# Gathers of V that wait for the logits' transposes, and a new set of engine orders

## The chip, the cores and the metric

The kernel runs on one core of one Trainium2 chip. The metric is the device time of one execution in microseconds (us); less is better. Five engines work side by side, each with its own in-order queue of instructions: TensorE (PE), ScalarE (ACT), VectorE (DVE), GpSimd (POOL) and SyncE (SP), which here only issues DMAs. They wait for one another, and for transfers, through semaphores.

## The reference, cut to what matters

```
xn = layernorm(x)                                   # x: 2048 rows of 512
# A: attention over 8 positions, each 2 rows apart, 32 heads of 16
q, k, v = split(xn @ wqkv)
logits[s,h,w] = 16**-0.5 * q[s,h] . k[s - 2*w, h]    # masked where s - 2*w < 0
A = (sum_w softmax_w(logits)[s,h,w] * v[s - 2*w, h]) @ wo
# B: a gated MLP with a product over the sequence
z = gelu(xn @ w_in);  z1 = z[:, :896];  z2 = layernorm(z[:, 896:])
g = w_sp @ z2 + b_sp                                 # w_sp: 2048 x 2048
B = (z1 * g) @ w_out
out = x + A + B                                      # bf16
```

## The kernel before, in words

All work is cut into some 800 named tasks. `build_kernel` declares them with what each reads and writes; from this come the dependencies. The order in which each engine runs its tasks is a written-out list, `ORDERS`, one for each of the five queues. An engine takes its tasks strictly in this order and, before each, waits for the tasks of other engines and the transfers that it depends on. A task that waits therefore holds up everything behind it on its engine.

The sequence has 16 blocks of 128 rows, in four groups `j` of four blocks. The stages, as PE sees them:

- **Front.** Per block: layer norm on DVE and POOL (`bnst`, `bnag`, `rstd`, `norm`), its transpose (`xTr` on PE, or `xTd`, a DMA transpose), then the products `z2_b_h` (the second half of `w_in`, halves h of 448 columns), `Qj_c`, `Kj_c` and `Vb`. ACT takes them out of PSUM: `z2g` (gelu), `z2s` (squares for the second layer norm), `QKe` and `halo` (Q and K), `Ve`. The V blocks go to a scratch tensor in DRAM, `vscr` (`Vw`, issued by SP).
- **Logits.** For each group, DVE multiplies Q with eight shifted copies of K (`prod`, `padd`), PE sums over the head (`lgj_0`, L707), and ACT copies the result to `stage` (`lgej`, L745). When all four groups are there, SP issues four DMA transposes `lgT0` to `lgT3` (L756) from `stage` to `attn`. `stage` lies on slots 15 to 22 of the buffer `Ve`.
- **z1.** Meanwhile PE makes the 32 half products `z1_b_h` (L807), through three pairs of PSUM banks, each freed by an ACT gelu `z1g` (L818). The z2 blocks are normalised in place, most on DVE (`zn`, L855), the last four on ACT (`zn12` to `zn15`, L851).
- **Softmax.** DVE and ACT compute it in two halves (even and odd blocks): `sm1` to `sm3` (maximum, L768 to L774), `ssub` (L780), `sexp` (L783, ACT), `sz1` to `sz3` (sum), `sln` and `srec` (ACT), `sattn` (L794). `sm1_0` is the first reader of `attn`.
- **Gate.** `w_sp @ z2` is done for eight pairs `i` of blocks with seven products instead of eight (Strassen's way): `P1_i` to `P7_i` (L930), each 8 matmuls of 128 x 448. They need sums of the z2 blocks made on DVE (`T1` L874, `T3` L877, `T2` L879, `T4` L881) and, for each pair, sums of the transposed `w_sp` blocks (`S13_i` L902, `S2_i` L905, `S4_i` L908); the blocks come by DMA transposes `wTi_h` (L892, SP). ACT copies the partial sums (`fk`, `S5`, `S2e`, `Sc`, `S3e`, `g11` to `g22`; L936, L958), and DVE multiplies with z1 (`u`).
- **V.** DVE multiplies the attention weights with the V rows (`pvb`, L1000) and adds up (`pva`, `pvc`). The V rows come back from `vscr` by nine gathers, `ldVp_k` (parity p, first slot k; L983), issued on ACT's queue. `ldV0_0` brings nine slots (1152 KB), `ldV1_7` eight (1024 KB), the others one or two.
- **Output.** DMA transposes `OTd` and `uT`, then `out_b` on PE (4 matmuls L1037 and 7 matmuls L1041), with x added through PSUM (`ldxr`, `os`), then `fin` and `st`.

PSUM ties the stages together: `P1_0` writes a bank that `z1g3` must have emptied, `P5_0` one of `z1g1`, `z1_5` one of `z1g11`.

Of the kernel before, what the change touches and what calls it, by code (L numbers as in the profile page):

```python
# [207 lines left out]
warm xTr0 fill0 z2_0_0 xTr1 z2_0_1 z2_1_0 xTr2 z2_1_1 xTr3 z2_2_0 z2_2_1 z2_3_0 Q0_0 K0_0 z2_3_1 K0_1 Q0_1 Q0_3
K0_2 Q0_2 K0_3 V0 V3 V1 V2 V4 V7 Q1_0 K1_0 V6 V5 K1_2 Q1_2 K1_1 Q1_1 Q1_3 z2_5_1 K1_3 z2_4_1 z2_4_0 z2_5_0
z2_6_1 z2_6_0 lg0_0 V9 V8 z2_7_1 z2_7_0 Q2_1 V11 K2_1 V10 Q2_0 K2_0 Q2_2 K2_2 z2_8_1 z2_8_0 K2_3 Q2_3 z2_11_0  # L210
z2_9_0 z2_9_1 z2_11_1 z2_10_1 z2_10_0 Q3_0 K3_0 V12 lg1_0 V15 K3_3 Q3_3 Q3_1 V13 K3_2 V14 K3_1 z2_14_1 z2_14_0
Q3_2 z2_12_1 z2_12_0 z2_13_0 z2_13_1 lg2_0 z2_15_0 z1_2_1 z2_15_1 z1_2_0 z1_0_0 z1_4_1 z1_4_0 z1_0_1 z1_8_1
# [8 lines left out]
actprime ldw_in2a_1 ldw_in2b_1 ldx3 xTe0 xTe1 z2g0 xTe2 xTe3 z2g1 z2g2 QKe0_0 halo0_0 z2g3 halo0_1 z2s0 QKe0_1
halo0_2 z2s1 QKe0_2 QKe0_3 z2s2 Ve3 halo0_3 Ve0 Ve1 Ve2 Ve7 Ve4 Ve6 Ve5 zm0 QKe1_0 QKe1_2 halo1_1 halo1_0
halo1_2 QKe1_1 z2s3 halo1_3 QKe1_3 z2g4 z2g5 z2s4 Ve9 Ve8 z2g6 lge0 z2g7 halo2_1 Ve11 QKe2_1 Ve10 z2s5 QKe2_0
z2s6 zm1 halo2_0 halo2_2 z2g8 halo2_3 QKe2_2 z2s7 QKe2_3 z2g11 z2g9 z2g10 QKe3_0 Ve12 Ve15 lge1 z2s8 z2s9 Ve13
# [5 lines left out]
S2e_4 srec1 fin0_0 os4_0 S3e_4 S5_4 g22_3 st0_0 Sc_4 g22_4 ldV1_6 ldxr10 g11_4 fin4_0 ldV1_2 g21_4 g11_5 S5_5  # L230
ldV1_4 os8_0 S2e_5 fin6_0 os10_0 S3e_5 st6_0 Sc_5 g12_4 fk_6 ldV1_0 S5_6 ldxr14 fin8_0 g12_5 st4_0 os12_0 g21_5
fin10_0 S2e_6 st10_0 os14_0 g22_5 ldxr15 S3e_6 st8_0 fin12_0 fk_7 os15_0 ldxr9 fin14_0 ldxr13 os13_0 st12_0 Sc_6
g21_6 ldxr11 g11_6 fin15_0 st14_0 S2e_7 g11_7 g22_6 ldxr7 g12_6 fin13_0 S5_7 S3e_7 os11_0 st15_0 st13_0 Sc_7
os9_0 ldxr5 ldxr3 g12_7 fin11_0 os7_0 fin9_0 os5_0 g21_7 g22_7 st11_0 fin7_0 ldxr1 os3_0 st7_0 st9_0 fin5_0
# [28 lines left out]

# [15 lines left out]
def build_kernel(nc, A_x, A_wqkv, A_wo, B_x, B_w_in, B_w_sp, B_b_sp, B_w_out, out,   # L279
# [82 lines left out]
    with ExitStack() as es:  # L362
# [391 lines left out]
        def lg_transposes():  # L754
            for n in range(4):
                dma("sp", (lambda n: lambda e: e.dma_start_transpose(  # L756
                    AC(off["attn"] + 1024 * n, [[128, 8], [1, 128]]), A("stage", 1024, 1024 * n)))(n),
                    128 * 1024 * 2, ("lgT", n), reads=["stage"] + [("lgs", j) for j in range(NJ)],
                    writes=[("attn", b) for b in range(4 * n, 4 * n + 4)], name="lgT%d" % n, xbar=True)
# [219 lines left out]
        def ld_v(par, k0, n):  # L979
            s0 = k0 + 8 * par  # L980
            src = bass.AP(tensor=vscr.tensor, offset=vscr.offset + (par + 2 * k0 + 2) * 512,
                          ap=[[16 * 512, 128], [1024, n], [1, 512]])
            dma("act", lambda e: e.dma_start(AC(off["Ve"] + 512 * s0, [[512, n], [1, 512]]), src), 128 * 512 * 2 * n,  # L983
                ("Ve", s0), reads=[("vscr", i) for i in range(-1, NB)], writes=[("Ve", s0 + i) for i in range(n)],
                name="ldV%d_%d" % (par, k0), prio=LOW)
# [201 lines left out]
```

## Time and profile before

| what | value |
|---|---|
| time, median of 3 runs | 232.52 us (231.87 to 236.08) |
| time of the profiled execution | 232.16 us |
| span of its profile | 230.4 us |
| PE busy | 221.3 us, 96% |
| DVE busy | 204.2 us, 89% |
| ACT busy | 147.6 us, 64% |
| POOL busy | 35.2 us, 15% |
| granted TensorE clock | full in every slice |
| DMA | 34.18 MB, mean 148 GB/s |

The span is from the first to the last instruction of the profile; the time has 1.8 us more around it. Times in the rows below are microseconds from the start of the span. A row of the order of time gives start, duration, engine, line and operation; a count such as x64 says that so many instructions in a row are merged. "SPq" and "ACTq" are the queues that issue DMAs. In brackets stands the idle time of the engine before the row and what ended it. Matmuls are pipelined: the end of one overlaps the start of the next.

### The profile page before, as it was taken

The page shows a single profiled execution, that of the slowest core. Times are in us where ns is not written, and L with a number is a line of the kernel's source. Part 1 is how long each engine was busy: PE and PEld are TensorE (multiplying, and loading weights), DVE is VectorE, ACT ScalarE, POOL GpSimd, SP SyncE. Part 2 cuts the span into 40 slices and gives each one's busy share as a digit, 9 for nine tenths or more (in the row PEclk, how much of TensorE's full clock was granted, in tenths as well). Part 3 has the DMA queues.
Part 4 walks back from the last instruction along what each step waited for, and adds up shares of the span by engine and source line. Part 5 has one row for each costly group of instructions (what it writes and reads, how often), then busy time and mean ns, then how long its engine had stood idle before and what let it go on. Part 6 is the DMA issues. An engine that isn't in the chain of part 4 may idle for free.

```text
span 230.4 us, 3073 instructions
## 1 busy us (share of the span) xinstructions
PE 221.3 (96%) x1128; PEld 115.6 (50%) x1142; DVE 204.2 (89%) x208; ACT 147.6 (64%) x258; POOL 35.2 (15%) x40
## 2 busy tenths in 40 slices
PE   7999999999999999949999899999999999999995
PEld 3454454455444776724455455454545444545443
DVE  4889999999999999639999999699999999999710
ACT  2579587788799796877993266349155525347562
POOL 2437304720370502011120000000000000000000
PEclk9999999999999999999999999999999999999999
DMA  6974631664309702970769952999999667827782
GB/s 190 318 243 48 182 90 49 177 145 87 84 20 163 176 1 48 170 216 24 182 190 170 254 137 55 167 216 232 211 227 193 169 120 175 154 68 171 165 180 68
DMA packets 84767, 34.18 MB, mean 148 GB/s; under 512 B 69280, under 2 KB 84400, under 8 KB 84752
## 3 DMA queue, kind: packets, MB, share of 16 engines
q1 hardware_dynamic: 74464, 23.78, 50.8%
q10 hardware_dynamic: 9408, 8.74, 13.2%
q0 software_dynamic: 880, 1.47, 2.2%
q8 instruction: 9, 0.15, 0.3%
q14 instruction: 6, 0.05, 0.1%
HBM read 12.98 MB, written 4.21 MB: 75 GB/s over the span
## 4 chain that ended last, share of the span: by engine, by line
PE 84%; DMA 8%; SPq 2%; DVE 2%; ACT 2%; issue 1%; DVEq 0%
PE ps L930 30%; PE ps L807 16%; PE ps L669 12%; PE ps L1041 10%; PE ps L646 6%; PE ps L1037 6%; DMA arena<-arena 5%; DMA arena<-in_B_w_sp_dram 3%; PE ps L567 2%; SPq L756 2%; ACT arena L818 1%; PE ps L707 1%; PE ps L619 1%; DVE arena L902 1%; DVE arena L879 0%
## 5 line engine op out<-in xcount | busy, mean ns | idle before, releaser
L930 PE MATMUL ps<-arena 128*128 128x448 bf16 x448 | 87.1, 352 | 4.0 <-DVE arena L855 3.2
L930 PEld LDWEIGHTS ps<-arena 128*128 128x128 bf16 x448 | 43.6, 98 | 46.2 <-issue 3.6
L807 PE MATMUL ps<-arena 128*128 128x448 bf16 x256 | 50.9, 353 | 0.1
L807 PEld LDWEIGHTS ps<-arena 128*128 128x128 bf16 x256 | 30.5, 121 | 18.6 <-issue 0.8
L694 DVE TENSOR_TENSOR arena<-arena 128x4096 bf16<-128x4096 bf16 x16 | 36.3, 2280 | 0.8 <-ACT arena L677 0.7
L1000 DVE TENSOR_TENSOR arena<-arena 128x4096 bf16<-128x4096 bf16 x16 | 36.2, 2286 | 0.2
L936 ACT ACTIVATE arena<-ps 128x448 bf16<-128x448 f32 x32 | 16.9, 539 | 28.7 <-PE ps L930 24.0
L818 ACT ACTIVATE arena<-ps 128x896 bf16<-128x896 f32 x32 | 28.7, 915 | 6.9 <-PE ps L807 6.8
L669 PE MATMUL ps<-arena 128*128 128x512 bf16 x123 | 29.2, 379 | 0.3
L1004 DVE TENSOR_TENSOR arena<-arena 128x4096 bf16<-128x4096 bf16 (+1 forms) x16 | 28.1, 1754 | 0.2
L698 DVE TENSOR_TENSOR arena<-arena 128x4096 bf16<-128x4096 bf16 x12 | 27.4, 2287 | 0.1
L1041 PE MATMUL ps<-arena 128*128 128x512 bf16 (+2 forms) x117 | 26.7, 366 | 0.1
L600 POOL TENSOR_TENSOR fpool<-fpool 128x1 f32<-128x1 f32 x16 | 18.9, 1189 | 26.0 <-DVE fpool L598 26.0
L669 PEld LDWEIGHTS ps<-arena 128*128 128x128 bf16 x128 | 14.5, 113 | 13.0 <-issue 0.2
L677 ACT ACTIVATE arena<-ps 128x1024 bf16<-128x1024 f32 x16 | 16.3, 1025 | 2.4 <-PE ps L669 2.4
L1041 PEld LDWEIGHTS ps<-arena 128*128 128x128 bf16 x119 | 11.4, 98 | 12.8
L958 ACT ACTIVATE arena<-arena,fpool 128x448 bf16<-128x448 bf16 x16 | 10.5, 664 | 9.5 <-DVE arena L953 9.5
L1037 PE MATMUL ps<-arena 128*128 128x512 bf16 (+2 forms) x62 | 15.3, 365 | 0.7 <-DMA arena<-arena 0.4
L826 ACT ACTIVATE arena<-arena 128x896 bf16<-128x896 bf16 x16 | 15.3, 955 | 0.1
L646 PE MATMUL ps<-arena 128*128 128x512 bf16 x63 | 15.3, 379 | 0.1
L1050 ACT ACTIVATE arena<-ps 128x512 bf16<-128x512 f32 (+1 forms) x16 | 9.4, 585 | 8.9 <-PE ps L1041 8.9
L843 POOL TENSOR_TENSOR fpool<-fpool 128x4 f32<-128x4 f32 x4 | 9.5, 2384 | 29.5 <-DVE fpool L840 29.5
(76 smaller groups left out, 186.7 us busy)
## 6 DMA issues: line engine op xcount, KB each, us to landing
arena<-in_A_x_dram ACTq DMA_DIRECT2D x17, 128.0 KB, 3.0
vscr<-arena SPq DMA_DIRECT2D x16, 128.0 KB, 1.9
arena<-in_A_x_dram SPq DMA_DIRECT2D x15, 128.0 KB, 2.7
out_dram<-arena ACTq DMA_DIRECT2D x15, 128.0 KB, 2.2
arena<-in_A_wqkv_dram SPq DMA_DIRECT2D x3, 512.0 KB, 4.6
arena<-vscr ACTq DMA_DIRECT2D x6, 256.0 KB, 3.7
arena<-vscr ACTq DMA_DIRECT2D x1, 1152.0 KB, 7.9
arena<-vscr ACTq DMA_DIRECT2D x1, 1024.0 KB, 7.0
```

Of the source, the lines that this page charges most:

```text
L600: T("pool", lambda g: g.tensor_tensor(Fv("rstd", 1, b), Fv("mv", 1, 2 * b + 1), Fv("mhalf", 1), ALU.pow), reads=[("mv", b), "mhalf"], writ ...
L646: last = t.matmul(bank(k + i), AC(off["xnT"] + dc * S + 128 * (b + i), [[1, 128]]), AC(off["wv_raw"] + 512 * dc, [[1, 512]]), start=(dc == ...
L669: last = t.matmul(bank(k + which), AC(off["wqk"] + 1024 * dc + col0, [[4, 128]]), AC(off["xnT"] + dc * S + 512 * j, [[1, 512]]), start=(dc ...
L694: T("dve", lambda v: v.tensor_tensor(pbv, qb, kb, ALU.mult), reads=[("QT", c, j), ("KT", c, j), ("KTpad", c, j)], writes=[("pb", s_)], est ...
L698: T("dve", lambda v: v.tensor_tensor(A("pb", 4096, 4096 * a), A("pb", 4096, 4096 * a), A("pb", 4096, 4096 * b), ALU.add), reads=[("pb", b) ...
L807: last = t.matmul(bank(k + hf, HF), AC(off["xnT"] + dc * S + t0, [[ts, 128]]), AC(off["w_in"] + 1792 * dc + c0, [[1, HF]]), start=(dc == 0 ...
L818: T("act", lambda a: a.activation(A(nm, FH, FH * b).rearrange("p (t n) -> p t n", t=2), PC(512 * k, [[512, 2], [1, HF]]), ACTF.Gelu_apprx_ ...
L930: last = t.matmul(bank(k, HF), AC(lo + 128 * s, [[1, 128]]), mov(s), start=(first and s == 0), stop=(s == 7), skip_group_check=True)
L1000: T("dve", (lambda iv, tv, av: lambda v: v.tensor_tensor(tv, iv, av, ALU.mult))(iv, tv, av), reads=[("attn", pairs[i][b]) for b in blks] + ...
L1004: T("dve", (lambda n: lambda v: v.tensor_tensor(AC(off["Vs"], [[4096, 2], [1, n]]), AC(off["Vs"], [[4096, 2], [1, n]]), AC(off["Vs"] + n, ...
L1037: t.matmul(po, AC(off["OT"] + 512 * os_ + 128 * cc, [[1, 128]]), AC(off["wo"] + 512 * cc + c0, [[1, n]]), start=False, stop=False, skip_gr ...
L1041: last = t.matmul(po, AC(off["uT"] + FH * us + 128 * fc, [[1, 128]]), AC(off["w_out"] + 512 * fc + c0, [[1, n]]), start=False, stop=(fc == ...
```

## The change

Two things change, and no computation is added or removed.

First, every gather `ldV` now also depends on all four transposes `lgT`: each transpose marks a key `lgTd`, which the gathers read. Among the gathers, `ldV1_7` had this dependency already, since its slots are those of `stage`.

Second, all five lists of `ORDERS` are replaced. The lines that bear on the stretch between the last logits and the first gate products are shown; the front and the second half are permuted in the same manner (for example, `out0_0` comes earlier among the products, `P5_2` and `P6_2` stand ahead of `P1_3`, and `ldw_in1` is issued later).

```diff
     pe="""
...
-z1_10_0 z1_6_1 z1_6_0 z1_8_0 z1_10_1 z1_12_1 z1_14_0 z1_14_1 z1_12_0 lg3_0 z1_15_0 z1_13_1 z1_11_1 z1_15_1
-z1_11_0 z1_13_0 z1_9_1 z1_9_0 z1_7_0 z1_7_1 z1_5_1 z1_3_1 z1_3_0 z1_1_1 z1_1_0 z1_5_0 P1_0 P1_1 P2_0 P5_0 P6_0
-P3_0 P6_1 P7_0 P2_1 P4_0 P1_2 P7_1 P5_1 P4_1 P2_2 P3_1 P1_3 P5_2 P6_2 P3_2 P5_3 P7_2 P2_3 P4_2 P6_3 P3_3 P7_3
...
+z1_6_1 z1_8_0 z1_8_1 z1_10_1 z1_10_0 z1_12_1 z1_12_0 z1_14_0 z1_14_1 lg3_0 z1_15_1 z1_15_0 z1_13_1 z1_13_0
+z1_9_1 z1_9_0 z1_7_1 z1_7_0 z1_11_1 z1_11_0 z1_3_1 z1_3_0 z1_1_0 z1_1_1 z1_5_1 P1_0 z1_5_0 P5_0 P2_0 P1_1 P6_0
+P3_0 P7_0 P2_1 P6_1 P5_1 P4_0 P7_1 P3_1 P1_2 P4_1 P2_2 P5_2 P6_2 P1_3 P7_2 P2_3 P4_2 out0_0 P3_2 P6_3 P5_3 P1_4
...
     act="""
...
-z1g10 lge2 z1g14 z1g12 lge3 zm2 z1g15 z1g13 z1g11 bspf z1g9 ldV0_0 z1g7 zn14 zn12 ldxr2 z1g3 zn13 z1g1 zn15 fk_0
-z1g5 sexp0 g11_0 S5_0 fk_1 os2_0 S2e_0 ldV0_11 ldxr8 sln0 srec0 Sc_0 S3e_0 sexp1 g22_0 S2e_1 g21_0 g11_1 fk_2
...
+z1g8 z1g10 z1g12 lge3 z1g14 z1g15 z1g13 zn13 z1g9 zn12 z1g7 ldxr0 z1g11 bspf ldV1_7 z1g3 zn14 zn15 z1g1 fk_0
+ldV0_0 z1g5 sexp0 fk_1 S5_0 S2e_0 sln0 Sc_0 srec0 S3e_0 S2e_1 S5_1 g11_0 g11_1 S3e_1 g12_0 g21_0 fk_2 Sc_1
...
     dve="""
...
-zq3 zv2 padd3_1 prod3_3 padd3_2 padd3_3 zv3 zn0 S13_0 zn2 zn1 smask zn7 zn3 zn11 zn10 S2_0 zn9 T1_0 S4_0 zn6 zn8
-T3_0 zm3 zn4 sm1_0 sm2_0 sm3_0 zn5 ssub0 T2_0 T1_1 T3_1 S13_1 T2_1 S2_1 sz1_0 sz2_0 S4_1 sm1_1 sz3_0 sm2_1 T4_0
-T4_1 sm3_1 ssub1 sattn0 h_0 pv2 pv0 u_0 pva2048_0 S13_2 pva1024_0 pvc0 S2_2 sz1_1 h_1 S4_2 S13_3 S2_3 pv6 sz2_1
...
+padd3_1 zq3 prod3_3 zv3 padd3_2 padd3_3 zn3 zn5 zn0 zn2 S13_1 zn11 zn1 S13_0 zm3 zn6 zn10 zn8 zn9 zn7 T1_0 zn4
+T1_1 sm1_0 T3_0 S2_0 S2_1 sm2_0 sm3_0 T3_1 ssub0 T2_1 S4_0 T2_0 T4_1 sz1_0 sz2_0 sz3_0 sm1_1 T4_0 sm2_1 S4_1
+sm3_1 ssub1 sattn0 h_0 pv0 pv2 pva2048_0 pva1024_0 pvc0 S13_2 S2_2 u_0 S4_2 sz1_1 h_1 pv4 sz2_1 S13_3 pv6 S2_3
...
     sp="""
...
-xTd14 xTd13 wT0_0 Vw8 Vw15 Vw14 wT1_1 wT0_1 Vw13 Vw12 wT1_0 lgT0 lgT3 lgT1 lgT2 wT2_0 wT2_1 wT3_0 wT3_1 uT_2
...
+Vw11 Vw8 wT1_1 ldw_in1 wT0_0 wT0_1 Vw15 Vw12 Vw14 wT1_0 Vw13 lgT0 lgT1 lgT3 lgT2 wT2_0 wT2_1 wT3_0 wT3_1 OTd0
...
@@ lg_transposes
-                    writes=[("attn", b) for b in range(4 * n, 4 * n + 4)], name="lgT%d" % n, xbar=True)
+                    writes=[("attn", b) for b in range(4 * n, 4 * n + 4)] + [("lgTd", n)], name="lgT%d" % n, xbar=True)
@@ ld_v
-                ("Ve", s0), reads=[("vscr", i) for i in range(-1, NB)], writes=[("Ve", s0 + i) for i in range(n)],
+                ("Ve", s0), reads=[("vscr", i) for i in range(-1, NB)] + [("lgTd", i) for i in range(4)], writes=[("Ve", s0 + i) for i in range(n)],
```

In the list of ACT, `ldV1_7` moves from between `fk_5` and `S2e_4` (the middle of the gate stage) to ahead of `z1g3`; `ldV0_0` moves from ahead of `z1g7` to behind `fk_0`.

More of the change, by code (lines that the diff above doesn't have):

```diff
@@ L207 @@
     pe="""
[L208 to L212, printed above, removed]
@@ L218 @@
-out9_0 P4_7 out7_0 out5_0 out3_0 out1_0 out1_1
+warm xTr0 fill0 z2_0_0 xTr1 z2_0_1 z2_1_0 xTr2 z2_1_1 xTr3 z2_2_0 z2_2_1 z2_3_0 z2_3_1 Q0_0 K0_0 Q0_1 Q0_2 K0_2
+K0_1 K0_3 V2 V1 V0 Q0_3 V7 V3 V4 V6 V5 Q1_0 K1_0 K1_1 Q1_2 Q1_1 Q1_3 K1_3 z2_4_1 K1_2 z2_6_1 z2_6_0 z2_4_0
+z2_5_0 z2_5_1 lg0_0 z2_7_1 z2_7_0 V10 V8 V11 V9 K2_0 Q2_0 K2_2 Q2_1 K2_1 Q2_2 K2_3 Q2_3 z2_8_1 z2_8_0 z2_9_0
+z2_9_1 z2_10_1 z2_10_0 z2_11_0 V13 z2_11_1 V14 lg1_0 V12 V15 K3_1 K3_0 Q3_0 K3_2 Q3_1 Q3_3 Q3_2 z2_12_0 z2_12_1
+K3_3 z2_13_1 z2_13_0 z2_14_1 z2_15_1 z2_14_0 lg2_0 z2_15_0 z1_0_0 z1_2_1 z1_0_1 z1_2_0 z1_4_0 z1_6_0 z1_4_1
@@ L219 @@
+P4_7 out9_0 out7_0 out5_0 out3_0 out1_0 out1_1
 """.split(),
     act="""
[L221 to L224, printed above, removed]
@@ L230 @@
[L230 to L234, printed above, removed]
@@ L235 @@
-os1_0 st5_0 fin3_0 st3_0 os1_1 fin1_0 st1_1
+actprime ldw_in2a_1 ldw_in2b_1 ldx3 xTe0 xTe1 z2g0 xTe2 xTe3 z2g1 z2s0 z2g2 z2g3 halo0_0 QKe0_0 QKe0_2 halo0_1
+QKe0_1 Ve2 halo0_2 Ve1 Ve0 QKe0_3 Ve3 halo0_3 Ve5 Ve6 Ve4 QKe1_0 halo1_1 z2s1 halo1_0 QKe1_1 Ve7 QKe1_3 halo1_3
+z2s2 QKe1_2 z2s3 halo1_2 z2g4 z2g6 z2g5 zm0 z2g7 z2s4 Ve8 Ve11 Ve10 Ve9 halo2_0 z2s5 QKe2_0 z2s6 halo2_2 QKe2_1
+lge0 halo2_1 QKe2_2 QKe2_3 halo2_3 z2s7 z2g8 z2g9 z2g10 z2s8 z2g11 Ve14 Ve13 lge1 Ve15 zm1 Ve12 z2s9 QKe3_0
+z2s10 QKe3_1 QKe3_2 z2g12 QKe3_3 z2s11 z2g13 z2s12 z2g14 zm2 z2s13 z2g15 z1g0 z2s14 z1g2 z2s15 z1g4 z1g6 lge2
@@ L236 @@
+g11_4 os10_0 fin8_0 ldV1_2 os12_0 S2e_5 g22_4 S5_5 ldV1_0 ldxr14 S3e_5 g11_5 st6_0 fin10_0 fk_6 ldxr15 g12_4
+fin12_0 st10_0 os14_0 Sc_5 st8_0 ldxr13 ldxr11 g22_5 S5_6 g12_5 g21_5 S2e_6 fin14_0 os15_0 Sc_6 st12_0 S3e_6
+st14_0 ldxr9 g11_6 g22_6 g12_6 os13_0 g21_6 fin15_0 fk_7 ldxr7 S5_7 os11_0 fin13_0 fin11_0 S2e_7 os9_0 st11_0
+ldxr5 ldxr3 S3e_7 st15_0 os7_0 Sc_7 g11_7 st13_0 ldxr1 g12_7 g22_7 g21_7 fin9_0 os5_0 st9_0 fin7_0 st7_0 os1_1
+os3_0 fin5_0 st5_0 os1_0 fin3_0 st3_0 fin1_0 st1_1
 """.split(),
@@ L248 @@
-pva1024_4 pvc4 pv9 pv11 pva2048_5 pva1024_5 S13_7 pvc5 S2_7 pv5 u_11 pv7 pva2048_6 pva1024_6 pvc6 S4_7 h_6 pv1
-pv3 u_7 pva2048_7 pva1024_7 h_7 pvc7 u_3 u_1 fin1_1
+zeros steps0 steps1 bnst0 bnag0 norm0 bnst1 bnag1 xTf0 norm1 bnst2 bnag2 bnst3 bnag3 norm2 bnst5 bnag5 norm3
+bnst7 bnag7 bnst8 bnst6 bnag6 bnst4 bnag8 norm7 bnag4 bnst9 bnst10 norm5 bnst11 norm6 norm4 bnag11 bnag9 bnag10
+prod0_0 prod0_2 prod0_1 norm8 padd0_1 bnst12 bnst13 padd0_2 prod0_3 norm11 bnst15 norm10 bnag15 bnag13 norm9
+bnag12 bnst14 padd0_3 bnag14 prod1_0 prod1_1 zq0 norm13 prod1_2 norm12 zq1 padd1_1 norm14 norm15 padd1_2 prod1_3
@@ new lines @@
+prod2_1 padd1_3 prod2_0 zv0 zv1 padd2_1 prod2_2 prod2_3 padd2_2 zq2 smask padd2_3 prod3_1 prod3_0 zv2 prod3_2
+padd3_1 zq3 prod3_3 zv3 padd3_2 padd3_3 zn3 zn5 zn0 zn2 S13_1 zn11 zn1 S13_0 zm3 zn6 zn10 zn8 zn9 zn7 T1_0 zn4
+T1_1 sm1_0 T3_0 S2_0 S2_1 sm2_0 sm3_0 T3_1 ssub0 T2_1 S4_0 T2_0 T4_1 sz1_0 sz2_0 sz3_0 sm1_1 T4_0 sm2_1 S4_1
+sm3_1 ssub1 sattn0 h_0 pv0 pv2 pva2048_0 pva1024_0 pvc0 S13_2 S2_2 u_0 S4_2 sz1_1 h_1 pv4 sz2_1 S13_3 pv6 S2_3
+pva2048_1 sz3_1 S4_3 u_4 h_2 pva1024_1 pvc1 pv8 pv10 S13_4 pva2048_2 u_8 h_3 pva1024_2 S2_4 pvc2 S4_4 sattn1
@@ L250 @@
+pv12 pv14 pva2048_3 pva1024_3 S13_5 pvc3 u_12 S2_5 pv13 h_4 pv15 S13_6 S4_5 pva2048_4 pva1024_4 S2_6 pvc4 pv9
+S4_6 pv11 h_5 pva2048_5 u_11 pva1024_5 u_15 pvc5 pv5 S13_7 h_6 pv7 S2_7 pva2048_6 u_7 pva1024_6 pvc6 S4_7 pv3
+pv1 pva2048_7 pva1024_7 pvc7 h_7 u_3 u_1 fin1_1
 """.split(),
     pool="""
-ktpad ident0 mhalf ident1 rstd0 rstd1 rstd2 rstd3 rstd6 mask0 mlog0 mask1 mlog1 mlog2 rstd4 rstd7 rstd5 rstd10
-rstd9 rstd8 rstd11 rstd13 rstd15 rstd12 rstd14 zr1 zr0 Vzero zr2 ldbsp zr3 ldwo0 ldwo1 ldwo2 ldwo3 ldwout
+ident0 mhalf ktpad ident1 rstd0 rstd1 rstd2 rstd3 rstd5 mask0 mlog0 mask1 mlog1 mlog2 rstd7 rstd6 rstd4 rstd10
@@ L260 @@
-uT_14 OTd5 uT_15 OTd6 uT_11 uT_9 uT_7 uT_5 OTd7 uT_3 uT_1 st1_0
+ldx0 ldx1 ldw_in2a_0 ldw_in2b_0 ldx2 ldx4 ldx5 ldx8 ldx6 ldx7 ldq ldk ldx9 ldx10 ldx11 ldwv xTd7 xTd5 xTd4 ldx15
+xTd6 ldx12 ldx14 Vw1 Vw2 ldx13 Vw0 xTd8 Vw3 Vw7 xTd11 xTd10 Vw4 Vw6 Vw5 xTd9 xTd12 xTd13 xTd14 xTd15 Vw9 Vw10
+Vw11 Vw8 wT1_1 ldw_in1 wT0_0 wT0_1 Vw15 Vw12 Vw14 wT1_0 Vw13 lgT0 lgT1 lgT3 lgT2 wT2_0 wT2_1 wT3_0 wT3_1 OTd0
+uT_0 wT4_0 uT_2 wT4_1 OTd1 uT_4 uT_6 wT5_0 uT_8 uT_10 OTd2 wT5_1 wT6_0 wT6_1 uT_12 OTd3 uT_14 OTd4 wT7_0 wT7_1
@@ L261 @@
+uT_15 uT_13 uT_11 uT_9 OTd5 uT_7 OTd6 uT_5 OTd7 uT_3 uT_1 st1_0
 """.split(),
```

21 lines of the change are left out of this document (6 added, 15 removed).

## The prediction

> **What bounds the kernel now.** I read the page's first part, then what TensorE waits for, then the order of time around its one long wait.
>
> ```profile
> span 230.4 us, 3073 instructions
> PE 221.3 (96%) x1128; PEld 115.6 (50%) x1142; DVE 204.2 (89%) x208; ACT 147.6 (64%) x258; POOL 35.2 (15%) x40
> ```
> TensorE (PE) is busy for 221.3 of 230.4 us. The diff adds and removes no matmul, so only its 9.1 us of idle time can change.
>
> The waits of PE, and one of VectorE (DVE); columns: total, times, longest:
>
> ```profile
> PE ps L930 <- DVE arena L855: 3.2, 1, 3.2
> PE ps L930 <- DMA arena<-in_B_w_sp_dram: 0.6, 1, 0.6
> PE ps L1037 <- DMA arena<-arena: 0.4, 1, 0.4
> PE ps L930 <- DVE arena L879: 0.2, 1, 0.2
> DVE arena L768 <- DMA arena<-arena: 5.6, 1, 5.6
> ```
> After its start PE stands still for 3.2 + 0.6 + 0.4 + 0.2 = 4.4 us in all; this is the most that any order can win. The rest of the 9.1 is start and end. The 3.2 is one wait for L855, a normalisation on DVE; and DVE itself waited 5.6 us in L768 (sm1_0, the first softmax step) for a transfer.
>
> The order of time (start, duration):
>
> ```profile
> 87.87 12.33 PE L807 MATMUL ps<-arena 128*128 128x448 bf16 x64
> 88.28 1.03 ACT L745 ACTIVATE arena<-ps 128x1024 bf16<-128x1024 f32 x1
> 89.34 5.91 SPq L756 DMA_TRANSPOSE arena<-arena  x4
> 94.34 0.40 ACTq L983 DMA_DIRECT2D arena<-vscr  x1
> 101.38 0.69 DVE L768 TENSOR_TENSOR arena<-arena 128x1024 bf16<-128x1024 bf16 x1 [5.58 <-DMA arena<-arena]
> 102.77 0.51 DVE L855 TENSOR_SCALAR arena<-arena,fpool 128x896 bf16<-128x896 bf16 x1
> 103.42 6.21 PE L930 MATMUL ps<-arena 128*128 128x448 bf16 x32 [3.23 <-DVE arena L855]
> 109.81 2.44 PE L930 MATMUL ps<-arena 128*128 128x448 bf16 x12 [0.17 <-DVE arena L879]
> ```
> From the chain, then the landings of L756 alone:
>
> ```profile
> 93.91 7.28 DMA arena<-arena
> 147.98 7.57 PE ps L930 x40
> DMA to landing us min/median/max: 3.2/3.5/7.3
> ```
> The chain reads: lge3 (L745) ends at 89.31; SyncE issues the four lgT transposes; the last, issued at 93.91, lands after 7.3 us at 101.2, where the four's median is 3.5. At 94.34, in the middle, ScalarE (ACT) issued the gather ldV0_0. sm1_0 waits for all four; zn5 (L855 at 102.77) stands behind sm1_0 in DVE's queue though it needs no logits; P1_0, PE's next product, needs zn5. So a late transfer costs PE 3.2 us through DVE's in-order queue.
>
> **The change, part by part.** *The gathers wait for lgT0 to lgT3.* Nothing can then share the DMA engines with the last transpose in the way ldV0_0 did. lge3 has less ahead of it on ACT (z1g14 is now behind it): L707's last products end at about 87.9, so it ends near 89.0, and the transposes start 0.3 us sooner. The last then lands at 93.6 + 3.5 = 97.1. Bounds: with the shortest landing (3.2) 96.8; if the collision is not what made it late, 100.9. I take L = 97.5, near the undisturbed end, 0.4 late because landings may queue.
>
> *The order of DVE.* zn5, T1_1 and S13_1 now stand ahead of sm1_0, so P1_0 no longer waits behind the softmax. Durations, by line, between 101.4 and 148.7 us (count, busy, mean ns):
>
> ```profile
> L768 DVE TENSOR_TENSOR arena<-arena 128x1024 bf16<-128x1024 bf16 x4 | 2.7, 686 | 5.6 <-DMA arena<-arena 5.6
> L780 DVE TENSOR_TENSOR arena<-arena 128x2048 bf16<-128x2048 bf16 x2 | 2.4, 1222 | 0.0
> L879 DVE TENSOR_TENSOR arena<-arena 128x1792 bf16<-128x1792 bf16 x2 | 2.2, 1084 | 0.0
> L905 DVE TENSOR_TENSOR arena<-arena 128x1024 bf16<-128x1024 bf16 x3 | 2.1, 687 | 0.0
> L908 DVE TENSOR_TENSOR arena<-arena 128x1024 bf16<-128x1024 bf16 x3 | 2.1, 684 | 0.0
> L771 DVE TENSOR_TENSOR arena<-arena 128x512 bf16<-128x512 bf16 x4 | 1.7, 423 | 0.1
> L877 DVE TENSOR_TENSOR arena<-arena 128x1792 bf16<-128x1792 bf16 x1 | 1.1, 1093 | 0.1
> L774 DVE TENSOR_TENSOR arena<-arena 128x256 bf16<-128x256 bf16 x2 | 0.6, 288 | 0.0
> ```
> From sm1_0 to T2_0, which P6_0 needs, the new order has sm1, T3_0, S2_0, S2_1, sm2, sm3, T3_1, ssub0, T2_1, S4_0, T2_0: 0.69 + 1.09 + 0.69 + 0.69 + 0.42 + 0.29 + 1.09 + 1.22 + 1.08 + 0.68 + 1.08 = 9.0 us. With sm1_0 at L + 0.2 = 97.7, T2_0 ends at 106.7.
>
> *The order of ACT, where the wait is added.* ldV1_7 now stands ahead of z1g3, and behind it are z1g3, zn14, zn15, z1g1, fk_0. It lies on the softmax's stage and so needs the lgT landed in any case; what is new is that ACT stands there until L. Rows for these:
>
> ```profile
> 96.51 2.15 ACT L851 ACTIVATE arena<-arena,fpool 128x896 bf16<-128x896 bf16 x2
> 98.56 0.91 ACT L818 ACTIVATE arena<-ps 128x896 bf16<-128x896 f32 x1
> ```
> The issue takes 0.4, so z1g3 runs 98.0 to 98.9, zn14 and zn15 until 101.1, z1g1 until 102.0. P1_0 needs z1g3 (its PSUM bank), P5_0 needs z1g1, P2_0 needs zn15, P6_0 needs T2_0.
>
> *The order of PE.* All z1 halves end at 100.2 now; one of them (z1_5_0, 12.33 / 16 = 0.77 us) moves behind P1_0, so P1_0 can start at 99.4. A product takes 7.57 / 5 = 1.51 us. Then P1_0 99.4 to 100.9 and z1_5_0 to 101.7; P5_0 waits 0.3 for z1g1, 102.0 to 103.5; P2_0 to 105.0; P1_1 to 106.6; P6_0 starts at 106.7, released by T2_0 almost at the moment PE reaches it. Before, the same work (all z1, then P1_0, P1_1, P2_0, P5_0) ended with P6_0 at 109.81. **PE is 3.1 us ahead there.** For other L: P6_0 starts at L + 9.2 as long as this is over 106.2; under L = 97.0 PE itself decides, and the lead stops at 3.6.
>
> *From P6_0 to the end.* The work is the same in another order: 228.06 - 109.81 = 118.25 us before (the last matmul of the chain ends at 228.06), which holds the 0.6 + 0.4 us of waits. Does DVE, the second busiest engine, keep up?
>
> ```profile
> 101.38:148.70 47.32, 45.26 (x47) 1.00 0.69 140
> 148.70:217.00 68.30, 67.47 (x53) 1.00 0.84 178
> 148.77 1.23 DVE L902 TENSOR_TENSOR arena<-arena 128x2048 bf16<-128x2048 bf16 x1 [1.61 <-DMA arena<-in_B_w_sp_dram]
> ```
> DVE has nothing free from 101.4 to 217 except the 1.6 us at S13_4. It starts this stretch 3.7 us sooner, with zn5, T1_1 and S13_1 (0.5 + 1.1 + 1.2) done and T3_0, S2_0, S4_0 (1.1 + 0.7 + 0.7) still to do, so it keeps some 4 us of lead and does not hold PE back on the mean.
>
> Single waits can return. S13_2, which P5_2 needs, waits for wT2_1, whose issue waits for P4_0:
>
> ```profile
> 119.09 9.12 SPq L892 DMA_TRANSPOSE arena<-in_B_w_sp_dram  x3
> DMA to landing us min/median/max: 4.4/5.2/7.6
> ```
> P4_0 ends near 117.5 in the new order, so wT2_1 lands between 121.9 and 125.1; P5_2 comes up at 125.2 and S13_2 takes 1.2 after the landing: a wait of 0 to 1.1. P1_3, which had the 0.6, now stands behind P5_2 and P6_2, 3 us later among the products, and its weights land sooner: that wait should go. I carry the same 1.0 us of waits as before, bounds 0 and 2.2 (twice as much and a little).
>
> *ldV1_7 early.* One megabyte of gather leaves the crowded second half (DMA share 0.84 above) for the stretch at 98 us. It hides behind the products; where it could collide is the third rival.
>
> *The front.* Up to lg3_0 PE has no wait now. The new order has a few thin places (z2_8_1 needs halo2_1, now behind lge0; z2_14_1 needs QKe3_3): laid end to end they leave 0.1 to 0.3 us. smask (0.3) and zv3 move ahead of padd3_3, and more normalisation is done while DVE waits for the first QKe. I cost the front at 0, bounds -0.2 and +1.
>
> *Sum.* 228.06 - 3.1 = 224.96 for the end of PE. The profiled execution took 232.16 with a span of 230.4; the tail is the same, so 232.16 - 3.1 = **229.1**. The runs shown have a median of 232.52, 0.4 above the profiled one; against it 229.1 is 1.5% less.
>
> **Rivals.** *Everything closes.* If the transposes land by 97.0 and no wait comes back, PE gains 3.6 + 1.0 = 4.6: 227.6. For it: T2_0 and P6_0 meet to a tenth. Against it: P5_0 behind z1g1, and thirty products in a new order with none waiting.
>
> *The change does not do what it says.* The last transpose is slow by itself, or because it is the fourth in a row. Then L = 100.9, z1g3 ends at 102.3, P5_0 starts at 105.4, P6_0 at 110.1: 232.4, no change. Against it: the other three landed within 3.2 to 3.8 (a median of 3.5 with the least at 3.2 leaves the third no more), and in the same 8 us the DMA engines moved this (0.2 us each, from 94 us):
>
> ```profile
> GB/s 216 218 206 209 178 117 128 191 173 108 163 137 73 33 100 166 129 326 328 361 320 328 352 352 356 371 380 356 348 318 323 276 292 343 348 256 67 26 20 49
> ```
> About 150 GB/s until 97.4, 340 after: the gather took the engines for itself until 101.2, when the last transpose's landing was told.
>
> *The gathers come late.* The place is pv0, DVE's first product with V, which needs ldV0_0. In the old order it lay ready for 16 us:
>
> ```profile
> arena<-vscr ACTq DMA_DIRECT2D x6, 256.0 KB, 3.7
> arena<-vscr ACTq DMA_DIRECT2D x1, 1152.0 KB, 7.9
> arena<-vscr ACTq DMA_DIRECT2D x1, 1024.0 KB, 7.0
> 118.47 4.49 DVE L1000 TENSOR_TENSOR arena<-arena 128x4096 bf16<-128x4096 bf16 x2
> ```
> Now ldV0_0 is issued at about 102.5, behind ldV1_7, and pv0 comes up near 115. At 340 GB/s both are in by 106; one after the other at their own rows 97.9 + 7.0 + 7.9 = 112.8: no cost. At the rate of the small gathers (256 KB in 3.7 us, 69 GB/s) it would be 129. DVE is full, so each us after 115 is lost to it, and to PE after 1.2 us of slack at S2_4; from 115 + 1.2 + 3.1 = 119.3 the change is a loss. At 125 it costs 8.8: 229.1 + 8.8 = 238. [...]
>
> **How the numbers follow.** Forecast 229.1, own range 227.9 to 230.6 (L from 97 to 98.3, waits of 0.5 to 1.5, the front): 0.55. Everything closes, 227.6: 0.22. No effect, 232.4: 0.15. Late gathers, 238: 0.08. The range 227.2 to 233.5 holds the first three and leaves out the fourth. About 2% is what a measurement of this kernel can tell from no change: under 227.9 is faster, over 237.2 slower. Faster: the closing case and the lower edge of the forecast, 0.25. Slower: the late gathers, 0.08. Within 2%: 0.67.
>
> **What would show it.** Right: the four lgT land within 4 us each; DVE's wait in L768 is under 2.5 us; PE's 3.2 us wait for L855 is gone; P6_0 starts near 106.7; PE's later waits come to about 1 us; the gathers land before 113. Wrong: a landing over 5 us of L756; DVE waiting for a vscr transfer in L1000; ACT's wait before z1g3 lasting beyond 99; or PE waits before lg3_0.

## The result, and the profile after

The changed kernel takes 228.93 us (median of 4 runs, 228.69 to 229.43); the kernel before, run beside it, 232.66 us (231.87 to 236.08). The ratio is 0.9854, with a 95% interval from 0.9821 to 0.9886: 1.5% faster. A run more than 1.5% above the fastest of its kernel counts as slow (here the one of 236.08), and the ratios are of the other runs alone. The profiled execution took 228.81 us with a span of 227.1, against 232.16 and 230.4: 3.35 us less.

The page's first part and what PE and DVE wait for, as shown of before:

```profile
span 227.1 us, 3070 instructions
PE 221.8 (98%) x1130; PEld 115.6 (51%) x1142; DVE 203.8 (90%) x208; ACT 147.8 (65%) x258; POOL 35.3 (16%) x40
...
PE ps L567 <- DVE fpool L494: 1.3, 1, 1.3
PE ps L930 <- ACT arena L818: 0.4, 1, 0.4
PE ps L930 <- issue: 0.2, 1, 0.2
PE ps L930 <- DVE arena L902: 0.2, 1, 0.2
PE ps L807 <- DVE arena L629: 0.2, 1, 0.2
...
DVE arena L768 <- DMA arena<-arena: 2.3, 1, 2.3
```
The work is the same. PE's 3.2 us wait for L855 and the 0.6 and 0.4 us waits for transfers are gone; behind the start's own (L567) no wait is over 0.4. DVE's wait in `sm1_0` fell from 5.6 to 2.3.

The order of time around that place:

```profile
89.52 6.22 SPq L756 DMA_TRANSPOSE arena<-arena  x4
98.31 0.69 DVE L768 TENSOR_TENSOR arena<-arena 128x1024 bf16<-128x1024 bf16 x1 [2.31 <-DMA arena<-arena]
98.49 0.60 ACTq L983 DMA_DIRECT2D arena<-vscr  x1
99.13 0.92 ACT L818 ACTIVATE arena<-ps 128x896 bf16<-128x896 f32 x1 [1.94 <-PE ps L807]
100.15 1.67 PE L930 MATMUL ps<-arena 128*128 128x448 bf16 x8 [0.23 <-issue]
101.86 0.39 ACTq L983 DMA_DIRECT2D arena<-vscr  x1
102.95 10.39 PE L930 MATMUL ps<-arena 128*128 128x448 bf16 x54 [0.37 <-ACT arena L818]
DMA to landing us min/median/max: 3.2/4.0/4.7
```
The last row is of L756 alone: no transpose of the logits takes more than 4.7 us, where one took 7.3. The last one lands at 98.19. `sm1_0` starts at 98.31, 3.1 us sooner than before; ACT issues `ldV1_7` (98.49) and `z1g3` follows at 99.13. The 1.94 in that row's bracket names PE, but the product that `z1g3` reads was long done: ACT stood at `ldV1_7` until the transposes had landed. `P1_0` starts at 100.15, right behind `z1g3` (before: 103.42); `ldV0_0` is issued at 101.86 and lands at 109.6. Inside the last PE row `P6_0` starts at 107.50 (before 109.81).

From there to the end (columns of the window: us, PE busy, granted clock, DMA share, GB/s; the share counts the whole time of every packet that starts in the window, so it can pass 1):

```profile
107.50:224.80 117.30, 116.67 (x597) 1.00 0.77 164
```
PE is busy for 116.67 of 117.30 us at the full clock; this part was 118.25 us long before.

### The profile page after: what moved, and what is told of

It reads as the page before. It is cut to its first block, busy times and chain, and to the rows that moved or that the text cites. A ratio compares the mean times of both kernels' runs of the same rounds, so it can differ in the third digit from the quotient of the medians.

```text
span 227.1 us, 3070 instructions
## 1 busy us (share of the span) xinstructions
PE 221.8 (98%) x1130; PEld 115.6 (51%) x1142; DVE 203.8 (90%) x208; ACT 147.8 (65%) x258; POOL 35.3 (16%) x40
## 4 chain that ended last, share of the span: by engine, by line
PE 85%; DMA 6%; SPq 3%; ACT 2%; DVE 2%; issue 1%; ACTq 0%; DVEq 0%
PE ps L930 33%; PE ps L807 15%; PE ps L669 12%; PE ps L1041 11%; PE ps L646 6%; PE ps L1037 6%; DMA arena<-in_B_w_sp_dram 3%; DMA arena<-in_A_x_dram 2%; SPq L756 2%; DMA arena<-arena 1%; ACT arena L818 1%; PE ps L707 1%; ACT arena L851 1%; DVE fpool L595 1%; DVE arena L902 1%
## 5 line engine op out<-in xcount | busy, mean ns | idle before, releaser
L930 PE MATMUL ps<-arena 128*128 128x448 bf16 x448 | 86.7, 352 | 0.8 <-ACT arena L818 0.4
L930 PEld LDWEIGHTS ps<-arena 128*128 128x128 bf16 x448 | 43.6, 98 | 42.9 <-ACT arena L818 0.8
L669 PE MATMUL ps<-arena 128*128 128x512 bf16 x126 | 28.5, 379 | 0.1
L669 PEld LDWEIGHTS ps<-arena 128*128 128x128 bf16 x128 | 14.5, 113 | 13.1
L646 PE MATMUL ps<-arena 128*128 128x512 bf16 x61 | 14.3, 379 | 0.2
L595 DVE BATCH_NORM_STATS2 fpool<-arena 128x6 f32<-128x512 bf16 x16 | 10.6, 676 | 3.2 <-DMA arena<-in_A_x_dram 3.1
```

The lines of the kernel that those rows point to most:

```text
L646: last = t.matmul(bank(k + i), AC(off["xnT"] + dc * S + 128 * (b + i), [[1, 128]]), AC(off["wv_raw"] + 512 * dc, [[1, 512]]), start=(dc == ...
L669: last = t.matmul(bank(k + which), AC(off["wqk"] + 1024 * dc + col0, [[4, 128]]), AC(off["xnT"] + dc * S + 512 * j, [[1, 512]]), start=(dc ...
L930: last = t.matmul(bank(k, HF), AC(lo + 128 * s, [[1, 128]]), mov(s), start=(first and s == 0), stop=(s == 7), skip_group_check=True)
```

## The experiments

The theory: a gather on the DMA engines while the four logits' transposes are under way makes the last one late, and the new orders turn an early end of the transposes into an early `P6_0`. The rivals: the last transpose is late anyway and the gain is DVE's new order (`zn5` ahead of `sm1_0`); or it is the added dependency itself; or the gain is made later, in the second half of the lists. In the diffs "..." stands for an unchanged part of a list. Where PE waits for several us, the times of one kernel spread from execution to execution, by 2.4 us in `gather_moved` and 9.0 in `both_moves`; so ranges stand with the medians, and the traces carry more than these.

### The dependency alone: wait_only, after_again

`wait_only` is the kernel before with the key `lgTd`; `after_again` is the changed kernel without it.

```diff
 wait_only (before, plus):
+  writes=... + [("lgTd", n)], name="lgT%d" % n
+  reads=... + [("lgTd", i) for i in range(4)], ... name="ldV%d_%d"
 after_again (after, less the same two additions)
```


> The orders of before, with the gathers waiting for the four transposes lgT. Theory (the gather ldV0_0 is what makes the last transpose late, and ACT's place of the wait is what it costs): the last lgT lands near 97.5 instead of 101.2, but ACT stands at ldV0_0, ahead of z1g7, until then. z1g7 ends at 98.9, zn14 and zn12 at 101.0, z1g3 at 101.9, z1g1 at 103.9, zn15 at 105.0, so P1_0 starts at 102.0, P2_0 at 105.6 and P6_0 at 108.6 (before 109.81): 231.4 us. Rival (the last transpose is slow by itself): it lands at 101.2, everything behind ldV0_0 on ACT is 3.7 later, P6_0 at 112.3: 236 us.

> The changed kernel without the key lgTd, that is, without the added dependency. In the new order ldV0_0 stands behind ldV1_7 on ACT, and ldV1_7 waits for all four lgT already, because its slots are those of stage. Theory: the added dependency makes no difference in the new order, 228.9 us. Rival (the dependency itself is what brings the gain): the collision returns, 232 us.

`wait_only`: 233.04 us (231.91 to 234.15, 10 runs) against 232.53 (13 runs), ratio 1.0016 (0.9982 to 1.0050): no gain, where 231.4 was expected. The transposes came undisturbed, 3.2 to 3.5 us each. But `ldV0_0` stands ahead of `z1g7`, `z1g3` and `z1g1` in ACT's old order, and ACT stood there until 99.43. PE's waits:

```profile
PE ps L930 <- DMA arena<-in_B_w_sp_dram: 1.9, 1, 1.9
...
PE ps L807 <- ACT arena L818: 1.2, 1, 1.2
```
The first is a new one at `P1_3`, the second the price of ACT's stand. In this execution the front was also late by 1.7 us (`lg3_0` at 89.02 instead of 87.32), so `P6_0` started at 110.05, and the single terms cannot be read cleanly from it.

`after_again`: 229.06 us (228.74 to 230.20, 6 runs) against 233.73 (29 runs), ratio 0.9817 (0.9774 to 0.9861): the whole gain without the dependency, as expected. (Its profiled execution was the slowest of the six, 230.20: `wT2_1` landed at 125.98 there and PE waited 1.6 us for `S13_2`.) In the new order `ldV0_0` stands behind `ldV1_7`, which waits for the transposes in any case. So the first half of the change does nothing here; the place in the list does it.

### The gather put back: gather_early

```diff
 ACT, after (without the key):
-z1g9 zn12 z1g7 ... z1g1 fk_0 ldV0_0 z1g5
+z1g9 zn12 ldV0_0 z1g7 ... z1g1 fk_0 z1g5
```


> The changed kernel without the added dependency, and with ldV0_0 moved back on ACT to ahead of z1g7, where it stood before. Theory (collision): the last lgT lands at about 101.5 again instead of 98.2; ACT stands at ldV1_7 until then, z1g3 ends at 103.0, z1g1 at 106.1, P5_0 starts at 106.1 and P6_0 at 110.7: 232.1 us. Rival (the new order as a whole brings the gain, the collision is harmless or absent): 228.9 us.

235.00 us (232.94 to 235.60, 12 runs), ratio 1.0050 (1.0013 to 1.0088): one moved instruction takes the whole gain away and 1.2 us more. L756 is L755 here, L930 is L929 (the rewritten list is a line shorter, also in the other kernels with L929). First the landings of L755 and PE's longest wait, then windows of PE across the wait (us, PE busy, granted clock, DMA share, GB/s):

```profile
DMA to landing us min/median/max: 4.7/6.5/9.8
...
PE ps L929 <- DVE arena L767: 4.5, 1, 4.5
...
100.00:102.00 2.00, 0.30 (x2) 1.00 1.26 228
102.00:104.00 2.00, 0.00 (x0) 0.72 0.28 61
104.00:106.00 2.00, 1.23 (x4) 0.50 0.57 161
106.00:108.00 2.00, 2.00 (x7) 0.50 0.98 337
108.00:110.00 2.00, 2.00 (x7) 0.57 0.08 26
110.00:112.00 2.00, 2.00 (x12) 1.00 0.17 21
```
`ldV0_0` was issued at 93.69 and the last transposes took up to 9.8 us; the last landed at 102.96. The row of the wait names `sm1_0` (L767), but `P1_0` reads nothing of the softmax: `z1g3`, held on ACT behind `ldV1_7` until 103.76, ended at 104.68, and `P1_0` started at 104.77. This is the collision made on purpose, with everything else as in `after_again`. 232.1 was expected, with `z1g3` ending at 103.0 and `P6_0` at 110.7; `P6_0` started at 114.00. Of these 3.3 us, 1.7 are there at the end of `z1g3`, since the last transpose landed 1.5 later than expected. The other 1.6 come behind it, where the granted clock was 0.50: from 102.88, inside the wait, until 109.70 (7 matmuls in 2 us, against 12 from 110 to 112). That term was in nobody's sum.

### One move alone, in the old orders: gather_moved, dve_order, both_moves

```diff
 gather_moved (ACT, before, no key):
-z1g9 ldV0_0 z1g7 ... zn15 fk_0 z1g5
+z1g9 z1g7 ... zn15 fk_0 ldV0_0 z1g5
 dve_order (DVE, before):
-zn4 sm1_0 sm2_0 sm3_0 zn5 ssub0 T2_0 T1_1 T3_1 S13_1 T2_1
+zn4 zn5 T1_1 S13_1 sm1_0 sm2_0 sm3_0 ssub0 T2_0 T3_1 T2_1
 both_moves: both
```


> The orders of before, with one task moved: ldV0_0 goes on ACT's queue from ahead of z1g7 to behind fk_0; no wait is added. Theory: the last lgT lands near 97.5, DVE starts sm1_0 at 97.7, zn5 is done at 99.6, so P1_0 starts at the end of z1 (100.2), P6_0 at 106.3, 3.5 ahead of before; the later waits of 1.0 us stay: 229.3 us. Rival (the order of DVE is what counts, and the transposes are slow by themselves): no change, 232.6 us.

> The orders of before, with three tasks moved on DVE: zn5, T1_1 and S13_1 go ahead of sm1_0. The gather is issued early as before. Theory: sm1_0 still waits until 101.4, but P1_0 starts at 100.2 without a wait for zn5; T2_1, which P6_0 needs, comes 0.5 + 1.1 + 1.2 us of DVE work sooner, at 107.2; P6_0 starts at 107.3, 2.5 ahead: 230.1 us. Rival (the late transfer sets P6_0 whatever stands in front of it): PE waits as long in front of P6_0 as it did in front of P1_0, 232.6 us.

> The orders of before, with ldV0_0 moved behind fk_0 on ACT and zn5, T1_1, S13_1 moved ahead of sm1_0 on DVE; no wait is added. Theory: both remove the same 3.2 us wait, so they don't add up: PE itself sets P6_0, at 106.3, 3.5 ahead, and the later waits of 1.0 stay: 229.1 us, at most 0.3 below the gather moved alone. Rival (they act on different waits): the gains add to 3.3 + 2.5, 227 us.

| kernel | us (range, runs) | last lgT landed | `P6_0` | `wT3_0` landed | wait at `P1_3` |
|---|---|---|---|---|---|
| before | 232.53 (231.62 to 235.65, 13) | 101.19 | 109.81 | 128.74 | 0.6 |
| gather_moved | 236.95 (235.57 to 237.98, 4) | 97.58 | 106.45 | 131.11 | 6.2 |
| dve_order | 235.12 (231.36 to 236.67, 4) | 100.33 | 106.44 | 130.96 | 6.1 |
| both_moves | 239.13 (234.51 to 243.55, 4) | 97.72 | 106.46 | 130.33 | 5.4 |
| after | 228.93 (228.69 to 229.43, 4) | 98.19 | 107.50 | 128.09 | none |

`gather_moved` has a ratio of 1.0188 (1.0130 to 1.0247): 1.9% slower. `dve_order` and `both_moves` have no ratio on record, since their four runs lie too far apart (ranges in the table). Up to `P6_0` `gather_moved` does just what the theory says, with 3.4 us of lead, more than the change itself. Its landings of L755, its order of time and its waits, then the windows at `P1_3`:

```profile
DMA to landing us min/median/max: 3.1/3.3/3.5
...
97.77 0.69 DVE L767 TENSOR_TENSOR arena<-arena 128x1024 bf16<-128x1024 bf16 x1 [1.60 <-DMA arena<-arena]
100.40 1.86 PE L929 MATMUL ps<-arena 128*128 128x448 bf16 x9
115.95 14.52 SPq L891 DMA_TRANSPOSE arena<-in_B_w_sp_dram  x3
...
PE ps L929 <- DMA arena<-in_B_w_sp_dram: 6.2, 1, 6.2
...
125.00:127.00 2.00, 0.00 (x0) 1.00 1.18 257
127.00:129.00 2.00, 0.00 (x0) 1.00 1.23 230
129.00:131.00 2.00, 0.00 (x0) 0.66 1.21 216
131.00:133.00 2.00, 1.85 (x6) 0.50 1.19 255
133.00:135.00 2.00, 2.00 (x7) 0.50 0.78 146
```
PE comes to `P1_3` at about 125 and stands until 131.15: the three `w_sp` transposes took SyncE 14.5 us to issue (9.1 before and after), 6.8 of it for `wT3_0` alone (2.9 before). The granted clock was 0.50 behind it. The spans say how 3.4 us of lead became 5.3 of loss (235.7 against 230.4): -3.4 at `P6_0`, +5.6 of wait (6.2 less 0.6), +2.7 of busy time for the same matmuls (224.0 against 221.3), 4.9 in all; 0.4 is not broken down.

`dve_order` reaches the same `P6_0` by the rival's way, with a late transpose (100.33), and in its profiled execution (235.26) loses it in the same place. So either move alone is enough for the early `P6_0`, and they do not add up, as expected (one profiled execution of each). 229 to 230 was expected of all three, and that failed: an early `P6_0` is not yet a gain. The loss is clear of the noise for `gather_moved` alone. The fastest run of `dve_order`, its only one at the full clock, took 231.36, 1.2 less than the median of before. The rival with the later part of the lists was right in so far as the new orders have to keep what the start of the stretch wins.

### Which later part keeps it: p13_first, both_wout_first

```diff
 p13_first (PE, after):
-P2_2 P5_2 P6_2 P1_3 P7_2
+P2_2 P1_3 P5_2 P6_2 P7_2
 both_wout_first (both_moves, and on POOL):
-ldwo0 ldwo1 ldwo2 ldwo3 ldwout
+ldwout ldwo0 ldwo1 ldwo2 ldwo3
```


> The changed kernel, with P1_3 put ahead of P5_2 on PE, so ahead of P5_2 and P6_2 as it stood before. Theory (the later waits left because P1_3 comes up after its weights have landed): P1_3 comes up at 125.7 and waits for wT3_0 until 128.1; 2.4 us of wait in the place of 0.2, and nothing behind it gives them back: 231.0 us. Rival (the products behind have slack towards other engines, PE catches up): at most 0.5 us, 229.4 us.

> The kernel of both_moves (orders of before, ldV0_0 behind fk_0, zn5, T1_1 and S13_1 ahead of sm1_0), with one more task moved: on POOL ldwout goes ahead of ldwo0. In both_moves PE gained its 3.3 us at P6_0 and then lost 5.4 us in front of P1_3, with wT3_0 landing at 130.3, and ran at half clock after that. Theory (the 896 KB of ldwout, pushed to 117 to 126 us by the chain of ldwo behind the gather, met wT2_1 and wT3_0): ldwout moves at 101 to 110, wT3_0 lands by 126, P1_3 waits under 1.5 us, the clock stays up: 230 us. Rival (the w_sp transposes meet the gather ldV0_9 and the other transposes there): wT3_0 still lands after 130, 235 us.

`p13_first`: 233.17 us (231.49 to 235.61, 12 runs), ratio 0.9977 (0.9945 to 1.0009): swapping one product with two others costs 4.2 us against the changed kernel, where 231.0 was expected. PE's waits and its windows:

```profile
PE ps L930 <- DMA arena<-in_B_w_sp_dram: 2.4, 1, 2.4
...
PE ps L930 <- ACT arena L936: 0.7, 1, 0.7
...
127.00:129.00 2.00, 1.09 (x6) 1.00 1.05 226
129.00:131.00 2.00, 2.00 (x8) 0.52 1.08 213
131.00:133.00 2.00, 2.00 (x8) 0.63 0.63 123
```
The wait has the size that was expected. What was not: the clock fell behind it, from 129.08 to 132.49 (the wait of 0.7 comes later, at 135.0). The granted clock, as a mean of the run, was full in 6 of the 12 runs (median 232.43) and lower in the other 6 (233.51); the 6 at the full clock are still 1.4 over what was expected, so the clock is not all of it. In the new orders, then, `P5_2` and `P6_2` ahead of `P1_3` are needed: they fill the time until `wT3_0` lands. Whether this place alone would make `gather_moved` a gain was not run.

`both_wout_first` tests whether `ldwout` (896 KB, issued by POOL) is what delays `wT3_0`: 233.58 us (232.01 to 234.74, 12 runs), ratio 1.0044 (1.0008 to 1.0081), where 230 was expected. `ldwout` went to 101.19 and `wT3_0` landed at 126.81 instead of 130.33: that part holds. But now `ldwout`, `ldV0_0` (until 113.03) and `ldwo1` (until 119.09) ran beside `wT2_0`, which landed at 118.86, and `P1_2` waited:

```profile
PE ps L929 <- DMA arena<-in_B_w_sp_dram: 2.7, 1, 2.7
```
The late landing moved from one block to another; which single transfer made `wT3_0` late in the old orders stays open.

### The other gather: v1_later, v1_mid, v1_mid_wout_first

```diff
 ACT, after:
-bspf ldV1_7 z1g3 zn14 zn15 z1g1 fk_0 ldV0_0 z1g5 ... Sc_4 ... fk_4 sln1
 v1_later:
+bspf z1g3 zn14 zn15 z1g1 fk_0 ldV0_0 ldV1_7 z1g5 ... fk_4 sln1
 v1_mid:
+bspf z1g3 zn14 zn15 z1g1 fk_0 ldV0_0 z1g5 ... fk_4 ldV1_7 sln1
 v1_mid_wout_first: v1_mid, with ldwout ahead of ldwo0 on POOL
```


> The changed kernel, with ldV1_7 moved on ACT from ahead of z1g3 to behind ldV0_0, which keeps its wait for the lgT. Theory: ACT no longer stands until 98.5, z1g3 and z1g1 come some 2 us sooner, and PE loses its waits in front of P1_0 (0.2) and P5_0 (0.4); then T2_0 at 107.0 sets P6_0, which starts 0.5 us sooner: 228.4 us. Rival: the gather ldV0_0 is no longer behind ldV1_7 and nothing else changes, since T2_0 was the true limit at P6_0: 228.9 us.

> The changed kernel, with ldV1_7 moved on ACT from ahead of z1g3 to behind fk_4, in the gate stage, near its place of before; ldV0_0 keeps its wait. Theory: as in v1_later PE loses its waits in front of P1_0 and P5_0 and P6_0 starts at 107.0; but without a second megabyte beside ldV0_0 the chain of ldwo and ldwout keeps its times of after (ldwout at 115 to 121), wT2_1 lands by 125, no wait over 1 us is left: 228.4 us. Rival (moving the gather pushes the later transfers into the w_sp transposes again): PE waits over 4 us near 127, 235 us.

> v1_mid with ldwout moved ahead of ldwo0 on POOL. Theory: ldwout shares the engines with ldV0_0 at 103 to 110 and is gone when the w_sp transposes come; wT2_1 and wT3_0 land as early as in after or sooner: 228.3 us, the fastest of all. Rival: ldV0_0 lands after 115 beside it and DVE waits in pv0, 230 us.

`v1_later`: 236.00 us (234.44 to 239.86, 12 runs), ratio 1.0081 (1.0045 to 1.0117), where 228.4 was expected. ACT no longer stands still, `P6_0` starts at 106.98 as expected; but the two large gathers now run at once, `ldV1_7` until 113.81, and everything queued behind them meets. The DMA issues between 114 and 130 us (count, KB each, median us to landing), first of `v1_later`:

```profile
arena<-in_B_w_out_dram POOLq DMA_DIRECT2D x1, 896.0 KB, 12.1
...
arena<-vscr ACTq DMA_DIRECT2D x1, 256.0 KB, 12.9
```
then of after:

```profile
arena<-in_B_w_out_dram POOLq DMA_DIRECT2D x1, 896.0 KB, 6.1
arena<-vscr ACTq DMA_DIRECT2D x1, 256.0 KB, 4.0
```
The same transfers took two to three times as long. `wT2_1` landed at 130.05 instead of 124.67, `S13_2` was late, and PE paid (with the granted clock at 0.50 again, from 128.45 to 135.28):

```profile
PE ps L929 <- DVE arena L901: 6.1, 1, 6.1
```
`v1_mid` puts `ldV1_7` into the middle of the gate stage, near its place in the old order: 228.53 us (228.09 to 228.76, 6 runs) against 232.97 (230.96 to 235.65, 23 runs), ratio 0.9821 (0.9784 to 0.9858); 228.4 was expected. PE's waits and two rows of its order of time:

```profile
PE ps L929 <- DVE arena L901: 1.1, 1, 1.1
PE ps L618 <- DVE arena L601: 0.4, 1, 0.4
...
99.61 1.68 PE L929 MATMUL ps<-arena 128*128 128x448 bf16 x8
```
ACT does not stand at the gather, `P1_0` starts at 99.61 and `P6_0` at 106.52; behind `S13_2` PE gives 0.9 of this 1.0 us back (1.1 of wait instead of 0.2), because `wT2_1` lands where it did (124.58). It has the lowest median of all kernels here, 0.4 under the changed kernel's, whose range it touches.

`v1_mid_wout_first`: 229.74 us (228.29 to 230.98, 6 runs), ratio 0.9871 (0.9824 to 0.9919), where 228.3 was expected. The profiled execution was the fastest (228.29; `wT2_1` at 123.47, 0.3 of wait left), but the runs spread; the earlier `ldwout` is no gain on the median.

### The clock by itself: before_filled

```diff
 before:
+filler(12, "fill1", 2600.0)      # 12 products of zeros, 128 x 512
 PE: -z1_5_0 P1_0    +z1_5_0 fill1 P1_0
```


> The kernel before, with 12 matmuls of zeros (128 x 512, into a PSUM bank that is free there) put on PE between z1_5_0 and P1_0, where it waits 3.2 us; they take 12 x 0.216 = 2.6 us and end before zn5 does. They add work that nothing reads. [...]

232.96 us (230.83 to 235.82, 12 runs) against 232.97 (23 runs), ratio 0.9997 (0.9958 to 1.0036). The filler was to keep PE busy through most of its wait, and the clock up (2.6 us for its 12 matmuls is an estimate: 1.51 / 8 us for one of 448 columns, from the prediction's rows, times 512 / 448). That this keeps the clock up was the author's estimate; no run shows how long a wait must be to bring it down: the clock was 0.50 behind a wait of 2.4 us in `p13_first` and full behind 3.2 us in the profile of before. The full clock is more frequent, in 9 of 12 runs against 7 of 23 of the kernel before beside it, but the median does not move: 232.0 was expected. The profiled execution, the slowest of the 12 (235.82), shows one reason: the last transpose, with the gather in its way as in before, landed at 104.58 (before 101.19), 2.7 us of the wait for `zn5` were left behind the filler, and the clock was at half for 3.41 us. Among the runs of before beside it, those at the full clock had a median of 231.64 (7), those at a mean of 0.993 233.13 (11), those at 0.985 234.99 (4). So here a lower clock goes with the slower runs, but this filler does not remove the spread; the landing of the last transpose is a likely source of it, and what else there is stays open.

## Why the prediction was right

Point by point, by its steps:

- *The transposes land undisturbed.* Right in kind: 4.7 us at most, no longer 7.3, and `gather_early` shows the cause (9.8 with the gather back). Over all fourteen profiles, the slowest of the four took 6.4 to 9.8 us in the four kernels that issue `ldV0_0` while they are under way (7.3 in before, 6.4 in `dve_order`, 9.8 in `gather_early`; and `before_filled`) and at most 4.8 in the ten others (4.8 in `v1_later`, 4.7 in after and `v1_mid`, 3.5 in `wait_only`, `gather_moved` and `both_moves`). L was 98.19 where 97.5 was taken: `lge3` ended at 89.49 instead of 89.0, and two of the four took 4.7 and 4.2 us, where under 4 was said of each. With no gather beside them the old orders have 3.6 at most (`wait_only`, `gather_moved`, `both_moves`, `both_wout_first`); why the new ones are slower there stays open.
- *The front at nothing.* `lg3_0` started 0.48 us later than before (87.80 against 87.32), within the bounds of -0.2 and +1.
- *DVE, from `sm1_0` to `T2_0`.* The chain was taken as 9.0 us; from 98.31 to the end of `T2_0` at 106.96 it took 8.65.
- *ACT standing at `ldV1_7`.* The steps are as worked out: `z1g3` follows at once (99.13), `z1g1` ends at 102.89 (102.0 by the smaller L), and `P5_0` waits 0.37 for it (0.3). But with the later L `z1g3` ended only at 100.05 and held back `P1_0` (100.15 instead of 99.4).
- *`P6_0`.* 107.50 instead of 106.7: the lead was 2.3, not 3.1. This term was 0.8 too large, by the front and the landings. They came through another path than the one named: `T2_0` was done at 106.96, so DVE did not release `P6_0`; PE itself was late, behind ACT's stand. In `v1_mid`, without that stand, `P6_0` started at 106.52.
- *From `P6_0` to the end.* 117.27 us, not 118.25: 1.0 us of later waits was carried, and 0.2 was there (at `P5_2`; `wT2_1` landed at 124.67, in the stretch forecast, and DVE waited 0.6 for it, but PE came up late enough). This term was 1.0 too long, 0.8 of it in the waits, and the 0.2 itself varies: in `after_again` the same place cost 1.6. The two errors cancel, so 229.1 met 228.8 better than its terms did; that is luck.
- *The rival that the change does nothing* (232.4) fell by the landings, and *the late gathers* (238) by `ldV0_0`: landed at 109.58, read at 115.35. *Everything closes* (227.6) failed by the lead, not by the later waits.

What the prediction did not see: it took the lead at `P6_0` as a gain and weighed later waits at 1 to 2 us. In the old orders the same lead turned into a loss of 4.4 us on the median (`gather_moved`). That the new lists behind `P6_0` hold it (`P1_3` behind `P5_2` and `P6_2` is the part shown) was in one sentence of it; the experiments make it half of the result. Nor is the clock in its sum. The profile of before that it read was at the full clock, but 53 of the 65 runs of before beside the experiments were under it, and none of the ten of the changed kernel and `after_again`: a usual run of before can have more to win than the 4.4 us of waits that the prediction called the most.

## What to carry to other kernels

Keep a large gather off the DMA engines while a transfer is under way whose end several engines wait for: here 8 us later cost nothing and 8 us earlier cost 6 us. Before you count a lead as a gain, look at what the engine runs into when it comes early, the next transfers above all; give it work to do until they land. Prefer the place in the list to a dependency when you place a transfer on an in-order queue: here the dependency alone won nothing (`wait_only`), because it held up what stood behind it, and the place won everything without it (`after_again`).
